# Buffers, transposes and normalisations of the first down stage in a fused attention and gated-MLP kernel

## The chip, the core and the metric

The kernel runs on one core of a Trainium2 chip. The core has five engines that run side by side and wait for one another by semaphores: TensorE (PE) for matmuls and transposes, VectorE (DVE) and ScalarE (ACT) for elementwise work, GpSimd (POOL) and SyncE (SP), which here mostly issue DMA transfers. The metric is the device time of one execution in microseconds (us), the median of several runs.

## The reference

```python
mod = (_silu(c) @ w_mod).reshape(c.shape[0], 6, 1, -1)
sa, ca, ga, sb, cb, gb = ...
h = _layernorm(x) * (1 + ca) + sa
x = x + ga * _A_ref(h, A_wqkv, A_wo)
h = _layernorm(x) * (1 + cb) + sb
x = x + gb * _B_ref(h, B_w_gate, B_w_up, B_w_down)
```

`x` is 2048 tokens by 576 in bfloat16. `_A_ref` is an attention of 32 heads of 18, in which a token sees itself and seven earlier tokens at a distance of two, with a softmax over these eight. `_B_ref` is a gated MLP: `((x @ w_gate) * (x @ w_up)) @ w_down`, 576 to 4608 and back.

## The kernel before

The tokens are cut in eight chunks of 256 for the attention and in tiles of 128 for the MLP. The MLP takes the tiles in five groups, of 2, 4, 4, 3 and 3 tiles (`GROUPS`), that is, group 0 is chunk 0 and group 1 is chunks 1 and 2. A group has a gate-up stage (`gate_up`), which makes `hh`, 36 tiles of 128 hidden features, and a down stage (`down`), which sums over those 36 rows `f`. The attention of the later chunks is laid between the matmuls of the MLP by lists written out by hand: the stage of group 0's down sums has `at0`, in which each piece of other work has the number of the row `f` behind which it is issued. TensorE, VectorE, ScalarE and the two issuing queues each execute in the order in which the code issues; nothing reorders.

The first down stage does this for two token tiles: per row `f` a matmul into `acc` (L840, 512 columns) and one into `accr` (L844, 64 columns) for each tile. Between the rows stand, for chunks 1 to 4:

- `gb_row`: the last gating row, and POOL's issues of `wd` blocks 1 and 2 and of chunk 2's neighbour values (`b_ld(2, 0)`, `b_ld(2, 1)`, L427, from `vd` into `vsh`);
- `a_ln`, `a_norm` (L262 to L272): the first layernorm of chunk 3 or 4, statistics and normalisation on VectorE, the reciprocal root on ScalarE (L267, L268); `a_norm` is followed by the load of a later chunk's rows (`load_x`, SP);
- `a_t` (L307, L294, L296): ten transposes of the normed chunk into two PSUM tiles, `tr_pA` (three of the five feature blocks) and `tr_pB` (two), and five modulated copies out of them into `hT`; the copies named in its second argument are VectorE's, the others ScalarE's. This transposed chunk is called T;
- `qkv_block(3)` (L529): chunk 3's projections, values first, and behind the values the reciprocal root of chunk 1's second layernorm;
- `av(n)`: the next `n` of chunk 2's 14 weighting pieces on VectorE; per token half four products with the attention (L501) and three pieces of sums (L508, twice, L510, L512), the last of which writes `o_sb`;
- `b_o` (L521, L523): the transposes of `o_sb` and ScalarE's copies into `oT`; `b_w(i, j)` (L685 to L688): the output projection of a token half into `pw` and `pwr`, which VectorE turns into the residual rows `x1`;
- `b_ln`, the normalisation of `x1`, and `b_t` (L307, L294, L296): the second layernorm and its T, into `h2T`, which group 1's gate-up reads. For chunk 2 the two halves go separately, `b_t(2, (0,))` behind the last row of the list and `b_t(2, (1,))` between the last sums.

All PSUM tiles, `acc`, `accr`, `pw`, `pwr`, `tr_pA`, `tr_pB`, `pp` and so on, come from one pool of eight banks; a tile that finds no free bank waits for the reader of an earlier one.

The nine blocks of `w_down` that the stage reads (four rows `f` each) come through three buffers (`wdp`). Block `f // 4 + 3` is issued by POOL behind the last row of block `f // 4`, once TensorE has read that block. The gate and up blocks of group 0 come through three buffers of `wgup` and, for its blocks 3, 4 and 8, two more of `wgx` that exist only up to the end of group 0 and that nothing uses in its down stage:

```python
wb = (wgx if g in (3, 4, NBLK - 1) else wgup).tile([P, KF, 2, NB], BF, name="wgu")
```

Of the kernel before, what the change touches and what calls it, by code (L numbers as in the profile page):

```python
# [7 lines left out]
BF = mybir.dt.bfloat16  # L8
# [10 lines left out]
P = 128  # L19
D = 576  # L20
# [26 lines left out]
def kernel(  # L47
# [112 lines left out]
    def load_wd(g):  # L160
        if g >= NG * NBLK - 4:
            return
        r0 = (g % NBLK) * FB * P
        wb = wdp.tile([P, FB, D], BF, name="wd")
        wd_blk[g] = wb
        return nc.gpsimd.dma_start(wb[:], B_w_down[r0:r0 + FB * P, :].rearrange("(k p) n -> p k n", p=P))  # L166

# [178 lines left out]
    def a_ln(i):  # L346
        x = x_in.pop(i)
        xn, rsq, norm = layernorm(lambda j: x[:, j, :], "a")
        aa[i] = dict(xn=xn, rsq=rsq, norm=norm)
# [16 lines left out]
    def a_t(i, on_dve=(0, 1, 2), between=None):  # L366
        a_tiles(i)
        hT = aa[i]["hT"]
        transposed(aa[i]["xn"], lambda m: hT[:, m, :], (0, 1), 0, between, KT if i in PAIRED else KF)(on_dve)
# [51 lines left out]
    def b_ld(i, j):  # L421
        b = bb.setdefault(i, dict(prod={}, vsh={}))
        base = HALO + i * CH + j * P - DIL * (W - 1)
        vsh = vshp.tile([P, W, DH, H], BF, name="vsh")
        vsrc = bass.AP(vd.tensor, vd.offset + base * D, [[D, P], [DIL * D, W], [1, D]])
        b["vsh"][j] = vsh
        return nc.gpsimd.dma_start(vsh[:].rearrange("p w d h -> p w (d h)"), vsrc)  # L427
# [180 lines left out]
    def qkv_block(i, between):  # L608
        q, k, qk4, v0_, v1_ = qkv_units(i, [(0, 0, 5)])[0]
        for pair in ((v0_, v1_), (q, k), (qk4,)):  # L610
            for part in range(2):
                for unit in pair:
                    unit[part]()
            if pair[0] is v0_:
                between()
# [60 lines left out]
    def b_w(i, j):  # L676
        pw = ps([P, 512], F32, "pw")
        pwr = ps([P, 64], F32, "pwr")
        parts = [(pwr, slice(512, D)), (pw, slice(0, 512))]
        if j == 0:  # L680
            parts.reverse()
        xt = x1p.tile([P, D], BF, name="x1")
        for p_t, cs in parts:
            for m in range(KT):
                nc.tensor.matmul(p_t[:], lhsT=oT[:, m, js(j)], rhs=wo[:, m, cs], start=(m == 0), stop=(m == KT - 1))  # L685
        for p_t, cs in parts:
            nc.vector.tensor_tensor(xt[:, cs], p_t[:], ga_bc[:, cs], ALU.mult)  # L687
        nc.vector.tensor_tensor(xt[:], xt[:], x_res[i][:, j, :], ALU.add)  # L688
        x1.setdefault(i, []).append(xt)

    def b_ln(i):
        x_res.pop(i)
        bb[i]["xn"], bb[i]["rsq"], bb[i]["norm"] = layernorm(lambda j: x1[i][j], "b")
# [11 lines left out]
    def b_t(i, cols=(0, 1)):  # L705
        ht, o0 = h2_of(ST * i + cols[0])
        transposed(bb[i]["xn"], lambda m: ht[:, m, o0:o0 + P * len(cols)], cols, 2)()
# [119 lines left out]
    def down(gi, hh, bg, late=nop):  # L827
        t0, t1 = GROUPS[gi]
        nj = t1 - t0
        final = gi == NG - 1  # L830
        last = FT - (2 if final else 1) * FB
        at = bg if gi == 0 else spread([(1.0, p) for p in bg], last)
        acc = [ps([P, 512], F32, "acc") for _ in range(nj - final)]
        halves = [(ps([P, CH], F32, "acc"), slice(CH * h, CH * (h + 1))) for h in range(2)] if final else []
        accr = ps([P, 2 * ST, 64], F32, "accr")

        def mm_a(f, j):
            wb = wd_blk[gi * NBLK + f // FB]
            for a, cs in [(acc[j], slice(0, 512))] if j < len(acc) else halves:
                nc.tensor.matmul(a[:], lhsT=hh[:, f, js(j)], rhs=wb[:, f % FB, cs], start=(f == 0), stop=(f == FT - 1))  # L840

        def mm_r(f, j):
            wb = wd_blk[gi * NBLK + f // FB]
            nc.tensor.matmul(accr[:, j, :], lhsT=hh[:, f, js(j)], rhs=wb[:, f % FB, 512:D],  # L844
                             start=(f == 0 and j == 0), stop=(f == FT - 1), skip_group_check=True)

        for f in range(last):
            for j in range(nj):
                mm_a(f, j)
                mm_r(f, j)  # L850
            if f % FB == FB - 1:
                load_wd(gi * NBLK + f // FB + 3)
            for piece in at[f]:
                piece()
        xs = [x1[t // ST][t % ST] for t in range(t0, t1)]
        if final:
            for j in range(nj):
                for f in range(last, FT - FB):
                    mm_r(f, j)
            for j in range(len(acc)):  # L860
                for f in range(last, FT - FB):
                    mm_a(f, j)
        for j in range(nj):
            for f in range(FT - FB, FT):
                mm_r(f, j)
        o_ts = [gup.tile([P, 512], BF, name="o_t", tag="g_sb" if j % 2 else "u_sb") for j in range(nj)]
        t_r = smp.tile([P, 2 * ST, 64], BF, name="t_r", tag="tree")
        nc.vector.tensor_tensor(t_r[:, 0:nj, :], accr[:, 0:nj, :],
                                gb_bc[:, None, 512:D].to_broadcast([P, nj, 64]), ALU.mult)
        if final:  # L870
            for j in range(nj):
                nc.vector.tensor_tensor(xs[j][:, 512:D], t_r[:, j, :], xs[j][:, 512:D], ALU.add)
            for j in range(nj):
                r0 = (t0 + j) * P
                for a, cs in [(acc[j], slice(0, 512))] if j < nj - 1 else halves:
                    for f in range(FT - FB if j < len(acc) else last, FT):
                        wb = wd_blk[gi * NBLK + f // FB]
                        nc.tensor.matmul(a[:], lhsT=hh[:, f, js(j)], rhs=wb[:, f % FB, cs], start=False, stop=(f == FT - 1))
                    nc.vector.tensor_tensor(o_ts[j][:, cs], a[:], gb_bc[:, cs], ALU.mult)
                    nc.vector.tensor_tensor(xs[j][:, cs], o_ts[j][:, cs], xs[j][:, cs], ALU.add)  # L880
                    stored = slice(0, CH) if cs.stop == CH else slice(cs.start, D)
                    nc.sync.dma_start(out_flat[r0:r0 + P, stored], xs[j][:, stored])
            return
        for j in range(nj):
            for f in range(last, FT):
                mm_a(f, j)
            if j == 0:
                late()
            nc.vector.tensor_tensor(o_ts[j][:], acc[j][:], gb_bc[:, 0:512], ALU.mult)
        for j in range(nj):  # L890
            r0 = (t0 + j) * P
            nc.vector.tensor_tensor(xs[j][:, 0:512], o_ts[j][:], xs[j][:, 0:512], ALU.add)
            nc.vector.tensor_tensor(xs[j][:, 512:D], t_r[:, j, :], xs[j][:, 512:D], ALU.add)
            nc.sync.dma_start(out_flat[r0:r0 + P, :], xs[j][:])
        load_wd(gi * NBLK + NBLK + 2)
# [267 lines left out]
    def gb_row():  # L1163
        mod_row(lambda p, k: wm5[p, k, :] if k < KF else wm5r[p, :], gb_bc, sc_bc2)()
        behind(load_wd(1), wgu_in[4])
        behind(b_ld(2, 0), wgu_in[7])
        place_pair_rows()
        load_wd(2)
        b_ld(2, 1)


    ln2 = []

    def last_ln(j):
# [5 lines left out]
        ln2[1](j)  # L1180
        ln2[2](slice(j, j + 1))

    def last_norm(j):
        ln2[3](j)

    def av(n):
        for p in av2[:n]:
            p()
        del av2[:n]

    at0 = [[] for _ in range(FT - FB)]
    for f, piece in ((0, gb_row), (0, lambda: a_ln(3)), (1, lambda: b_o(1)), (2, lambda: av(2)), (3, lambda: (a_norm(3), load_x(5))),
                     (4, lambda: b_w(1, 0)), (5, lambda: av(2)), (6, lambda: a_t(3, (0,))), (7, lambda: b_w(1, 1)), (8, lambda: av(2)),
                     (9, lambda: b_ln(1)), (10, lambda: av(1)), (11, lambda: qkv_block(3, bb[1]["rsq"])), (11, lambda: bb[1]["norm"]()), (12, lambda: av(4)),
                     (13, lambda: b_t(1)), (15, lambda: av(3)), (19, lambda: a_ln(4)), (22, lambda: b_o(2)), (23, lambda: (a_norm(4), load_x(6))),
                     (25, lambda: b_w(2, 0)), (25, lambda: last_ln(0)), (26, lambda: b_w(2, 1)), (26, lambda: last_ln(1)), (27, lambda: a_t(4, (0,))),
                     (30, lambda: last_norm(0)), (30, lambda: last_norm(1)), (31, lambda: b_t(2, (0,)))):
        at0[f].append(piece)

    dbg = {0: at0,  # L1200
# [44 lines left out]
```

## Time and profile before

| | |
|---|---|
| median of 3 runs | 556.63 us (556.52 to 557.35) |
| the profiled execution | 556.8 us, of which the span from the first to the last instruction is 555.1 us |
| TensorE busy | 543.2 us, 98% of the span |
| VectorE, ScalarE, POOL busy | 329.5 us (59%), 254.5 us (46%), 65.8 us (12%) |
| TensorE clock granted | full speed in all 40 slices of the span |
| moved by DMA | 108.40 MB, mean 195 GB/s |
| first down stage | about 88.3 to 126.6 us of the span |

A row of a timeline gives start and duration in us, engine, line, operation, output and inputs by the program's names and shapes, and the number of instructions merged in it; a bracket at its end tells how long the engine was idle before it and what ended the idle time. A row of the waits gives who waited for whom, the total, how often. A row of stretches gives the stretch, then the busy time of TensorE's matmuls, its weight loads, VectorE, ScalarE and POOL with the number of instructions, the granted clock, the DMA share and GB/s. A row of DMA issues gives the transfer, the issuing queue, the size and the time to landing.

### The profile page before, as it was taken

The numbers are of one execution on the slowest core, as the hardware profiler recorded it, in microseconds if no ns is written. First come the engines' busy times: TensorE is split into PE (matmuls) and PEld (weight loads), VectorE is DVE, ScalarE is ACT, GpSimd is POOL, SyncE is SP. The second block draws the span as 40 slices with busy tenths as digits, with TensorE's granted clock in tenths as the row PEclk, the third lists the DMA queues.
The fourth block names the chain that finished last, engine by engine and source line by source line (L and its number), as shares of the span: only waits on it lengthen the run. The fifth ranks groups of instructions, "written<-read, shape, count | busy, mean of one in ns | idle before, by whom it ended". The sixth has DMA issues, their size and how long they took to land.

```text
span 555.1 us, 14848 instructions
## 1 busy us (share of the span) xinstructions
PE 543.2 (98%) x6283; PEld 326.2 (59%) x6317; DVE 329.5 (59%) x795; ACT 254.5 (46%) x604; POOL 65.8 (12%) x98
## 2 busy tenths in 40 slices
PE   8999999989999999999999999999999999999997
PEld 5787886656544465555544445556655555565564
DVE  7888899887369763556267786444627615322202
ACT  2746665535555664212655554113556511455500
POOL 3102213121000001112000100111100022200010
PEclk9999999999999999999999999999999999999999
DMA  8999999567345844336734775435585665976021
GB/s 271 278 279 318 346 316 345 201 198 275 100 151 178 286 140 137 109 123 184 250 85 151 230 223 184 125 97 165 168 290 192 193 191 179 322 223 188 1 86 33
DMA packets 70156, 108.40 MB, mean 195 GB/s; under 512 B 3690, under 2 KB 57850, under 8 KB 70090
## 3 DMA queue, kind: packets, MB, share of 16 engines
q1 hardware_dynamic: 58832, 61.50, 36.8%
q0 software_dynamic: 11168, 45.81, 25.8%
q8 instruction: 49, 0.80, 0.6%
q14 instruction: 17, 0.14, 0.1%
q10 hardware_dynamic: 90, 0.15, 0.1%
HBM read 103.00 MB, written 4.44 MB: 194 GB/s over the span
## 4 chain that ended last, share of the span: by engine, by line
PE 83%; DMA 9%; DVE 3%; issue 2%; ACT 1%; POOL 0%; SPq 0%; POOLq 0%
PE pg L529 28%; PE pu L529 22%; PE acc L840 19%; PE pp L529 5%; PE accr L844 3%; DMA wgr<-in_B_w_gate_dram 3%; PE pw L685 2%; DMA wo<-in_A_wo_dram 2%; PE lg L448 2%; DMA wgu<-in_B_w_gate_dram 1%; DMA x_t<-in_A_x_dram 1%; DMA wd<-in_B_w_down_dram 1%; DMA wmA<-in_w_mod_dram 1%; ACT hT L296 1%; PE tr_pA L307 0%
## 5 line engine op out<-in xcount | busy, mean ns | idle before, releaser
L529 PE MATMUL pg<-h2T,wgu 64*128 64x512 bf16 (+2 forms) x1440 | 279.9, 333 | 0.0
L529 PE MATMUL pu<-h2T,wgu 64*128 64x512 bf16 (+2 forms) x1440 | 279.1, 333 | 0.0
L529 PEld LDWEIGHTS <-wgu 64*128 64x128 bf16 x2880 | 141.2, 94 | 103.1
L796 ACT CAST u_sb<-pu 128x512 bf16<-128x512 f32 (+2 forms) x180 | 90.1, 500 | 127.9 <-PE pg L529 125.9
L802 DVE TENSOR_TENSOR hh<-g_sb,u_sb 128x512 bf16<-128x512 bf16 (+2 forms) x180 | 66.7, 372 | 113.0 <-ACT g_sb L797 111.1
L840 PE MATMUL acc<-wd,hh 128*128 128x512 bf16 (+1 forms) x523 | 130.2, 372 | 1.2 <-DMA wd<-in_B_w_down_dram 1.0
L844 PE MATMUL accr<-wd,hh 128*128 128x64 bf16 x528 | 93.7, 193 | 1.1
L797 ACT CAST g_sb<-pg 128x512 bf16<-128x512 f32 (+2 forms) x180 | 91.4, 508 | 0.0
L840 PEld LDWEIGHTS <-hh 128*128 128x128 bf16 x588 | 55.2, 98 | 60.3 <-issue 1.7
L529 PE MATMUL pg<-h2T,wgr 64*128 64x512 bf16 (+2 forms) x180 | 60.1, 334 | 0.7 <-ACT h2T L296 0.5
L529 PE MATMUL pu<-h2T,wgr 64*128 64x512 bf16 (+2 forms) x180 | 60.2, 334 | 0.0
L166 POOL DMA_DIRECT2D wd<-in_B_w_down_dram x41 | 30.8, 751 | 236.0 <-PE accr L844 212.0
L844 PEld LDWEIGHTS <-hh 128*128 128x128 bf16 x576 | 51.8, 98 | 2.7 <-issue 1.1
L501 DVE TENSOR_TENSOR vsh<-vsh,attn 128x1152 bf16<-128x1152 bf16 x56 | 40.4, 750 | 0.0
L438 DVE TENSOR_TENSOR prod<-qT,kT 128x1280 bf16<-128x1280 bf16 x46 | 36.6, 816 | 4.3 <-ACT kT L364 4.3
L529 PEld LDWEIGHTS <-wgr 64*128 64x128 bf16 x360 | 17.8, 94 | 16.6 <-issue 4.1
L427 POOL DMA_DIRECT2D vsh<-vd x14 | 12.5, 897 | 109.5 <-DVE o_sb L512 71.8
L687 DVE TENSOR_TENSOR x<-pw,ga_bc 128x512 bf16<-128x512 f32 x14 | 9.7, 689 | 26.5 <-PE pw L685 26.5
L267 ACT ACTIVATE ln_rstdb<-ln_mvb,eps 128x2 f32<-128x2 f32 (+1 forms) x10 | 3.0, 299 | 46.9 <-DVE ln_mvb L264 46.9
L294 DVE TENSOR_SCALAR h2T<-tr_pA,modc 128x128 bf16<-128x128 bf16 (+1 forms) x30 | 9.5, 371 | 24.7 <-PE tr_pA L307 24.7
L296 ACT ACTIVATE h2T<-tr_pB,modc 128x256 bf16<-128x256 bf16 (+1 forms) x18 | 8.2, 518 | 30.2 <-PE tr_pB L307 30.2
L529 PE MATMUL pp<-hT,wqk 64*128 64x256 bf16 x360 | 22.0, 269 | 0.0
(220 smaller groups left out, 555.4 us busy)
## 6 DMA issues: line engine op xcount, KB each, us to landing
wd<-in_B_w_down_dram POOLq DMA_DIRECT2D x41, 576.0 KB, 4.6
wgu<-in_B_w_gate_dram SPq DMA_DIRECT2D x45, 512.0 KB, 4.6
wgu<-in_B_w_up_dram SPq DMA_DIRECT2D x45, 512.0 KB, 5.8
vsh<-vd POOLq DMA_DIRECT2D x14, 1152.0 KB, 8.9
x_r<-in_A_x_dram SPq DMA_DIRECT2D x8, 288.0 KB, 7.0
vsh<-in_B_w_down_dram POOLq DMA_DIRECT2D x4, 576.0 KB, 9.0
out_dram<-x SPq DMA_DIRECT2D x15, 144.0 KB, 4.5
x_t<-in_A_x_dram SPq DMA_DIRECT2D x7, 288.0 KB, 6.0
```

The source lines that it names most:

```text
L166: return nc.gpsimd.dma_start(wb[:], B_w_down[r0:r0 + FB * P, :].rearrange("(k p) n -> p k n", p=P))
L296: nc.scalar.activation(dst, s, ACTF.Identity, bias=modc[:, vi_shift, m:m + 1], scale=modc[:, vi_scale, m:m + 1])
L427: return nc.gpsimd.dma_start(vsh[:].rearrange("p w d h -> p w (d h)"), vsrc)
L438: nc.vector.tensor_tensor(prod[:], aa[i]["qT"][:], aa[i]["kT"][:, :, off:off + CH], ALU.mult)
L448: nc.tensor.matmul(b["lg"][H * wl:H * (wl + 1), wq, :], lhsT=ind[:, m, :], rhs=b["prod"][4 * wq + wl][:, m, :], start=(m == 0), stop=(m == ...
L501: nc.vector.tensor_tensor(v, v, at, ALU.mult)
L529: return nc.tensor.matmul(dst, lhsT=lhs, rhs=rhs, start=first, stop=last, skip_group_check=True)
L796: nc.scalar.copy(u[:, 0:N], pu[:, 0:N])
L797: nc.scalar.copy(g[:, 0:N], pg[:, 0:N])
L802: nc.vector.tensor_tensor(hh[:, f, 0:N], g[:, 0:N], u[:, 0:N], ALU.mult)
L840: nc.tensor.matmul(a[:], lhsT=hh[:, f, js(j)], rhs=wb[:, f % FB, cs], start=(f == 0), stop=(f == FT - 1))
L844: nc.tensor.matmul(accr[:, j, :], lhsT=hh[:, f, js(j)], rhs=wb[:, f % FB, 512:D], start=(f == 0 and j == 0), stop=(f == FT - 1), skip_grou ...
```

## The change

Three things are changed, all in the first down stage. The `w_down` blocks 3, 4 and 8 of group 0 go into buffers of `wgx` rather than `wdp`. Blocks 3 and 4 are issued in `gb_row`, and the blocks issued behind rows 3, 7, 11 and 15 are then 5, 6, 7 and 8; behind rows 19 and 23 nothing is issued, and from row 27 on it is as before. T of chunks 3 and 4 is copied out by ScalarE alone. T of chunk 1 is cut in two: the transposes behind row 11 (`turn`), its copies behind row 15, behind chunk 2's last sums. With that most pieces of `at0` move by some rows: both `b_w` of chunk 1 stand together ahead of `a_t(3)` at row 4, `qkv_block(3)` is at row 10, the weighting is cut 2, 2, 2, 5, 3, and `a_norm(4)` stands behind `b_w(2, 0)`.

```diff
 def load_wd(g):
...
-        wb = wdp.tile([P, FB, D], BF, name="wd")
+        wb = wgx.tile([P, FB, D], BF, name="wgu") if g in (3, 4, NBLK - 1) else wdp.tile([P, FB, D], BF, name="wd")
...
-            if f % FB == FB - 1:
-                load_wd(gi * NBLK + f // FB + 3)
+            if f % FB == FB - 1 and (gi > 0 or f // FB not in (4, 5)):
+                load_wd(gi * NBLK + f // FB + (5 if gi == 0 and f // FB < 4 else 3))
...
 def gb_row():
...
         load_wd(2)
+        load_wd(3)
         b_ld(2, 1)
+        load_wd(4)
...
+    turned = []
+
+    def turn(i):
+        ht, o0 = h2_of(ST * i)
+        turned.append(transposed(bb[i]["xn"], lambda m: ht[:, m, o0:o0 + CH], (0, 1), 2))
...
-                     (4, lambda: b_w(1, 0)), (5, lambda: av(2)), (6, lambda: a_t(3, (0,))), (7, lambda: b_w(1, 1)), (8, lambda: av(2)),
-                     (9, lambda: b_ln(1)), (10, lambda: av(1)), (11, lambda: qkv_block(3, bb[1]["rsq"])), (11, lambda: bb[1]["norm"]()), (12, lambda: av(4)),
-                     (13, lambda: b_t(1)), (15, lambda: av(3)), (19, lambda: a_ln(4)), (22, lambda: b_o(2)), (23, lambda: (a_norm(4), load_x(6))),
-                     (25, lambda: b_w(2, 0)), (25, lambda: last_ln(0)), (26, lambda: b_w(2, 1)), (26, lambda: last_ln(1)), (27, lambda: a_t(4, (0,))),
-                     (30, lambda: last_norm(0)), (30, lambda: last_norm(1)), (31, lambda: b_t(2, (0,)))):
+                     (4, lambda: b_w(1, 0)), (4, lambda: b_w(1, 1)), (4, lambda: a_t(3, ())), (5, lambda: av(2)), (8, lambda: b_ln(1)), (9, lambda: av(2)),
+                     (10, lambda: qkv_block(3, bb[1]["rsq"])), (10, lambda: bb[1]["norm"]()), (11, lambda: av(5)), (11, lambda: turn(1)),
+                     (15, lambda: av(3)), (15, lambda: turned.pop()()), (17, lambda: a_ln(4)), (19, lambda: b_o(2)), (22, lambda: b_w(2, 0)),
+                     (22, lambda: (a_norm(4), load_x(6))), (23, lambda: last_ln(0)), (23, lambda: b_w(2, 1)), (25, lambda: a_t(4, ())),
+                     (26, lambda: last_ln(1)), (30, lambda: last_norm(0)), (30, lambda: last_norm(1)), (31, lambda: b_t(2, (0,)))):
```

## The prediction

> **What bounds the kernel now.** I read the page, then TensorE's (PE's) waits, then the timelines of the first down stage, which is the only place whose code moves.
>
> ```profile
> span 555.1 us, 14848 instructions
> PE 543.2 (98%) x6283; PEld 326.2 (59%) x6317; DVE 329.5 (59%) x795; ACT 254.5 (46%) x604; POOL 65.8 (12%) x98
> ...
> PE pg L529 <- DMA wgu<-in_B_w_gate_dram: 0.2, 1, 0.2
> ...
> 88.30:126.60 38.30, 34.88 (x378) 21.88 (x381) 34.14 (x91) 17.67 (x51) 8.95 (x13) 1.00 0.74 235
> ```
>
> TensorE sets the time: 98% busy. Of its few waits behind the start all but the last in this list (0.2, the first gate-up block's) lie between 88.3 and 126.6 us, the stage that the change rewrites. There VectorE (DVE, the third figure of the stretch) is busy 34.14 of 38.30 us, so it is the next limit. The stage's fixed points on TensorE, in its timeline:
>
> ```profile
> 88.37 0.39 PE L840 MATMUL acc<-wd,hh 128*128 128x512 bf16 x1
> 92.61 1.24 PE L685 MATMUL pw<-wo,oT 128*128 128x512 bf16 x5
> 93.84 0.38 PE L840 MATMUL acc<-wd,hh 128*128 128x512 bf16 x1
> 95.43 0.34 PE L307 MATMUL tr_pA<-ident,ln_xn 128*128 128x128 bf16 x3
> 99.37 0.19 PE L844 MATMUL accr<-wd,hh 128*128 128x64 bf16 x1
> 100.48 2.38 PE L529 MATMUL pp<-wv,hT 64*128 64x288 bf16 x36 [0.92 <-ACT hT L296]
> 107.62 0.39 PE L840 MATMUL acc<-wd,hh 128*128 128x512 bf16 x1
> 109.17 0.38 PE L840 MATMUL acc<-wd,hh 128*128 128x512 bf16 x1
> 113.58 0.61 PE L521 MATMUL oT_pA<-ident,o_sb 128*128 128x128 bf16 x8
> 115.82 0.38 PE L840 MATMUL acc<-wd,hh 128*128 128x512 bf16 x1 [1.03 <-DMA wd<-in_B_w_down_dram]
> 116.80 1.24 PE L685 MATMUL pw<-wo,oT 128*128 128x512 bf16 x5
> 123.44 0.34 PE L307 MATMUL tr_pA<-ident,ln_xn 128*128 128x128 bf16 x3 [0.53 <-DVE ln_xn L272]
> 126.60 0.37 PE L529 MATMUL pg<-h2T,wgr 64*128 64x512 bf16 x1 [0.47 <-ACT h2T L296]
> ```
>
> In brackets is the idle time and who ended it. An accr's row lasts 0.19 but the next matmul starts some 0.03 behind it, so each bracket hides 0.16 more: 0.92 + 1.03 + 0.53 + 0.47 + 4 x 0.16 = 3.6 us, and 0.35 at the transposes near 95.43. That is 3.95 us to be had. The remaining 38.23 - 3.95 = 34.28 us is issue time that the change only reorders. Its units: a row f 0.49 (109.17 to 113.58 is nine), a b_w 1.23 (92.61 to 93.84), chunk 3's qkv block 7.14 (100.48 to 107.62); a b_o or a pair of transposes 0.56, gb_row 1.22.
>
> **Part 1: T of chunk 3, and a new wait.** Both b_w of chunk 1 now stand at f = 4, ahead of a_t(3). Eight PSUM banks: acc, acc, accr hold three, the two b_w four more, so tr_pA takes the last and tr_pB must wait until VectorE has emptied chunk 1's first pw. In VectorE's order that copy stands behind a_norm(3), and nothing ahead of it is changed:
>
> ```profile
> 95.49 0.68 DVE L687 TENSOR_TENSOR x<-pw,ga_bc 128x512 bf16<-128x512 f32 x1
> 96.72 1.42 DVE L501 TENSOR_TENSOR vsh<-vsh,attn 128x1152 bf16<-128x1152 bf16 x2
> 98.50 1.02 ACT L296 ACTIVATE hT<-tr_pA,modc 128x256 bf16<-128x256 bf16 x2 [4.74 <-DVE hT L294]
> ```
>
> TensorE comes to tr_pB at 92.61 + 2 x 1.23 + 0.17 = 95.24; the bank is free at 96.17 + 0.06. New wait: 0.99. Queued behind it on TensorE is everything, f = 5 on; ScalarE (ACT) waits too. In exchange hT no longer waits 4.74 for VectorE's one copy: ScalarE does all five, some 0.46 apart (two take 1.02, one 0.56) from 96.7, when tr_pA is full, and is ready at 99.1. TensorE ends a_t(3) at 96.62 and f = 10 six rows later, at 99.56, so the 0.92 wait goes. The qkv block ends at 106.70, f = 11 at 107.19: 0.43 ahead of the 107.62 for the same work.
>
> **Part 2: chunk 1's T and the sums.** VectorE's norm of chunk 1 keeps its distance to the qkv block, since ScalarE copies the values first:
>
> ```profile
> 104.25 1.19 DVE L272 TENSOR_SCALAR ln_xn<-x,ln_mvb,ln_rstdb 128x576 bf16<-128x576 bf16 x4 [0.22 <-ACT ln_rstdb L268]
> 105.34 2.76 DVE L501 TENSOR_TENSOR vsh<-vsh,attn 128x1152 bf16<-128x1152 bf16 x4
> 109.26 1.05 DVE L294 TENSOR_SCALAR h2T<-tr_pA,modc 128x256 bf16<-128x256 bf16 x3 [1.16 <-PE tr_pA L307]
> 112.47 0.46 DVE L512 TENSOR_TENSOR o_sb<-vsh 128x576 bf16<-128x576 bf16 x1
> ```
>
> 104.25 - 100.48 = 3.77, so it starts at 103.33 and ends 104.42; the last two adds of token half 0 now follow. All four adds of a half take 2.7 (110.23, where the copies end, to 112.93), these two an estimated 1.2 of it. The products start at 105.62 and take 2.7, the adds 2.7: o_sb is complete at 111.05. That is 1.9 earlier than 112.93, mostly because the 1.16 wait and 0.97 of h2T copies no longer stand between products and adds. TensorE: turn(1) 107.19 to 107.75, eight rows to 111.67, then b_o(2), whose second transpose needs o_sb: slack 0.6. turn(1)'s two banks are held until VectorE copies them at 112.0; b_o's two bring the held ones to seven, so that costs nothing.
>
> **Part 3: the buffers.** Only the order of the transfers on POOL's queue changes. The issues before, then the times to landing of the first three and of the one at 110.61:
>
> ```profile
> 90.53 0.76 POOL L166 DMA_DIRECT2D wd<-in_B_w_down_dram  x1 [5.69 <-PE pb L332]
> 91.28 0.89 POOL L427 DMA_DIRECT2D vsh<-vd  x1
> 92.58 0.76 POOL L166 DMA_DIRECT2D wd<-in_B_w_down_dram  x1 [0.41 <-PE accr L844]
> 96.67 0.75 POOL L166 DMA_DIRECT2D wd<-in_B_w_down_dram  x1 [3.33 <-PE pwr L685]
> 110.61 0.76 POOL L166 DMA_DIRECT2D wd<-in_B_w_down_dram  x1 [5.79 <-PE accr L844]
> ...
> wd<-in_B_w_down_dram POOLq DMA_DIRECT2D x1, 576.0 KB, 6.6
> vsh<-vd POOLq DMA_DIRECT2D x1, 1152.0 KB, 9.3
> wd<-in_B_w_down_dram POOLq DMA_DIRECT2D x1, 576.0 KB, 10.1
> wd<-in_B_w_down_dram POOLq DMA_DIRECT2D x1, 576.0 KB, 5.2
> ```
>
> They land at 97.1, 100.6, 102.7 and 115.8: in issue order, 3.5 us for 1152 KB (337 GB/s), 2.1 for 576. Block 6's issue at 110.61 had waited behind the qkv block; that is the 1.03 (1.19) stall. After, blocks 3, 4 and 5 go out by 94.4, block 6 behind f = 7 (98.1), block 7 behind f = 11 and the value stores (107.3, landing 112.5, used at 119), block 8 behind f = 15 (109.7, landing 115, used at 121); no down block is late. What moves back is b_ld(2,1), behind block 3: by 2.1 us, to 102.7, or 103.6 with x's load beside it, against 105.62 when the products need it: 2 us of cover. load_x(6) on SP moves with a_norm(4) to about 117.5; nothing follows it there until the stores. That matmuls read three blocks from other buffers costs nothing: the last stage reads vsh buffers at wd's pace.
>
> **Part 4: the tail.** TensorE, unhindered: b_o(2) ends 112.23, three rows to 113.70, b_w(2,0) to 114.93, a row, b_w(2,1) to 116.65, two rows, a_t(4) 117.63 to 118.19, six rows to 121.13. VectorE's chain starts 1.28 into b_w(2,0), as before:
>
> ```profile
> 118.08 0.69 DVE L687 TENSOR_TENSOR x<-pw,ga_bc 128x512 bf16<-128x512 f32 x1 [0.86 <-PE pw L685]
> 122.69 0.36 DVE L294 TENSOR_SCALAR hT<-tr_pA,modc 128x256 bf16<-128x256 bf16 x1
> 122.96 1.31 DVE L272 TENSOR_SCALAR ln_xn<-x,ln_mvb,ln_rstdb 128x576 bf16<-128x576 bf16 x4
> 125.20 0.85 DVE L294 TENSOR_SCALAR h2T<-tr_pA,modc 128x128 bf16<-128x128 bf16 x3
> 120.53 0.29 ACT L267 ACTIVATE ln_rstdb<-ln_mvb,eps 128x1 f32<-128x1 f32 x1 [4.53 <-DVE ln_mvb L264]
> 122.80 0.29 ACT L267 ACTIVATE ln_rstdb<-ln_mvb,eps 128x1 f32<-128x1 f32 x1 [1.75 <-DVE ln_mvb L264]
> 125.03 1.51 ACT L296 ACTIVATE h2T<-tr_pB,modc 128x128 bf16<-128x128 bf16 x4
> ```
>
> From 114.98 it takes 4.61 (118.08 to 122.69) plus 1.15 for a_norm(4) (1.19 in the row at 104.25, less the overlap), which now stands inside it; the hT copy at 122.69 is gone. Norm of half 0: 120.74 to 121.35, so the transposes wait 0.28, to 121.41. For half 1 ScalarE is late: it starts the first rstd at 118.6 (120.53 is 2.45 into the chain, and 1.15 more), has it 0.5 later, then does five hT copies to 121.4, then the second rstd (0.53) to 121.95. That is the price of T on ScalarE alone. Norm of half 1 ends 122.62; from there to the end of the last h2T copy it took 126.05 - 124.19 = 1.86, so 124.48, and the gate-up starts at 124.54. TensorE alone would be there at 121.41 + 2.53 = 123.94.
>
> **Sum.** 124.54 against 126.60: 2.06 us. The waits: gone 0.35 + 1.08 + 1.19, the last two 1.31 shrink to 0.28 + 0.60, new 0.99; 3.93 - 1.87 = 2.06. After 126.6 TensorE waits for nothing (the 0.2 above is the first gate-up block's), and all later loads are paced by it, so I carry the gain through. The profiled execution took 556.8 us, 0.17 above the median 556.63: forecast 554.7 for it, 554.6 at the median. Bounds: if neither the bank nor the tail holds (0.99 + 0.88), 552.7; I lean far to the chain, whose rows are this stage's own, hence 553.6 below.
>
> **Rivals.** A, slower: b_ld(2,1) late. If transfers of the queue share the engines rather than follow one another, it lands with the last. Behind 97.1 stand four down blocks (0.59 MB each), its 1.18, x's 0.29 and the value stores' 0.29: 4.1 MB (sizes by the code), at 337 GB/s until 109.3, at the stage's mean of 235 until 114.5. Every microsecond past 106.2 (105.62 and the slack of 0.6) is added; from 108.3 the gain is gone, from 109.4 it is measurably slower: 557.7 to 562.9, say 558.5. Against it: the landings in issue order above. Chance 0.06.
>
> B, VectorE held up by POOL: two more issues (1.5 us) move into 91.3 to 94.4, ahead of a_norm(3) and the bank. Held for all of it, the new wait is 2.5 and the time 556.1. Rows: the two products at 96.72, beside an issue at 96.67, took 1.42; the four at 105.34, with no issue, 2.76, so 0.04 per issue. Chance 0.05. The Trainium skill's page "GPSIMD Engine Reference", section "1. Specifications", speaks for B: POOL shares its SBUF interfaces with VectorE, with contention where VectorE has two SBUF inputs, as these products have. By that rule up to 1.5 us of the gain would go; the trace shows 0.04 an issue.
>
> C, no change: the gain is given back after 126.6 by a load that comes no earlier. Against it: no such wait of TensorE before. 556.6, chance 0.07.
>
> D, more: bank or tail wait absent, near 553.3, chance 0.06. The forecast has 0.76.
>
> **Chances.** Faster by over 0.2% (1.1 us, about what can be told from no change): forecast and D, 0.82; within: B and C, 0.12; slower: A, 0.06. The range 553.6 to 556.3 holds the forecast, most of D and B.
>
> **What would show it.** A wait of TensorE of about 1 us at a_t(3)'s tr_pB behind VectorE's x copy, no wait at the qkv block, none for wd, a wait of 0.3 before b_t(2) and 0.6 before the first gate-up of group 1, which starts near 124.5. Wrong if b_o(2) waits for o_sb, or if the qkv block starts after 100.

## The result and the profile after

| | before | after |
|---|---|---|
| median of 16 runs | 556.67 us (556.26 to 558.63) | 554.59 us (553.93 to 556.94) |
| ratio after to before | | 0.9961, 95% interval 0.9951 to 0.9971 |
| the profiled execution, its span | 556.8 us, 555.1 us | 554.21 us, 552.5 us |

The changed kernel is faster by 2.08 us at the median; the interval of the ratio is 1.6 to 2.7 us. The two profiled executions lie 2.6 us apart, within that interval.

The page of the kernel after, its list of TensorE's waits from 84 us on (who waited for whom, total, times, longest), and the busy time over the stage, in the columns explained for the kernel before:

```profile
span 552.5 us, 14851 instructions
PE 542.6 (98%) x6284; PEld 326.7 (59%) x6317; DVE 328.9 (60%) x793; ACT 255.5 (46%) x606; POOL 64.8 (12%) x98
...
PE tr_pB L307 <- DVE x L687: 0.8, 1, 0.8
PE accr L844 <- issue: 0.2, 1, 0.2
...
88.30:124.60 36.30, 35.07 (x385) 22.29 (x388) 32.98 (x88) 18.66 (x53) 11.25 (x15) 1.00 0.82 261
```

The three waits shown for the old stage are gone (hT at the projections, a `w_down` block, the norm ahead of the second T) and the one for h2T at the gate-up no longer shows in the list. One new wait is there, 0.76 at `tr_pB`. (The 0.2 at `accr` is put down to no other engine: it stands behind the projections, where the record of one matmul into `acc` is missing from the trace.) These are the stage's fixed points on TensorE, its timeline in the kernel after:

```profile
92.66 1.24 PE L685 MATMUL pw<-wo,oT 128*128 128x512 bf16 x5
95.11 0.33 PE L307 MATMUL tr_pA<-ident,ln_xn 128*128 128x128 bf16 x3
96.20 0.27 PE L307 MATMUL tr_pB<-ident,ln_xn 128*128 128x128 bf16 x2 [0.76 <-DVE x L687]
...
99.71 2.38 PE L529 MATMUL pp<-wv,hT 64*128 64x288 bf16 x36
111.83 0.61 PE L521 MATMUL oT_pA<-ident,o_sb 128*128 128x128 bf16 x8
113.86 1.24 PE L685 MATMUL pw<-wo,oT 128*128 128x512 bf16 x5
121.28 0.33 PE L307 MATMUL tr_pA<-ident,ln_xn 128*128 128x128 bf16 x3
122.94 1.03 PE L840 MATMUL acc<-wgu,hh 128*128 128x512 bf16 x4
124.00 0.37 PE L529 MATMUL pg<-h2T,wgr 64*128 64x512 bf16 x1
```

The gate-up of group 1 starts at 124.00 instead of 126.60. From the first `b_w` of chunk 1 to this start the stage takes 31.34 (124.00 - 92.66) against 33.99 (126.60 - 92.61). I use this length, called the stage below, for all kernels, since the profiled executions reach its start up to 1 us apart. The gain of 2.60 (126.60 to 124.00) is carried to the end unchanged. These two rows are the last matmuls of the program in the timelines of the kernel before and after:

```profile
547.93 3.42 PE L878 MATMUL acc<-vsh,hh 128*128 128x512 bf16 x23
```

```profile
545.33 3.42 PE L878 MATMUL acc<-vsh,hh 128*128 128x512 bf16 x23
```

### The profile page after: what moved, and what is told of

It reads as the page before. It is cut to its first block, busy times and chain, and to the rows that moved or that the text cites. A ratio compares the mean times of both kernels' runs of the same rounds, so it can differ in the third digit from the quotient of the medians.

```text
span 552.5 us, 14851 instructions
## 1 busy us (share of the span) xinstructions
PE 542.6 (98%) x6284; PEld 326.7 (59%) x6317; DVE 328.9 (60%) x793; ACT 255.5 (46%) x606; POOL 64.8 (12%) x98
## 4 chain that ended last, share of the span: by engine, by line
PE 88%; DMA 9%; DVE 2%; issue 1%; ACT 0%; SPq 0%
PE pg L529 28%; PE pu L529 22%; PE acc L840 21%; PE pp L529 6%; PE accr L844 4%; DMA wgr<-in_B_w_gate_dram 3%; PE pw L685 2%; DMA wo<-in_A_wo_dram 2%; PE lg L448 2%; DMA wgu<-in_B_w_gate_dram 1%; DMA x_t<-in_A_x_dram 1%; DMA wmA<-in_w_mod_dram 1%; PE tr_pA L307 1%; PE tr_pB L307 0%; PE oT_pA L521 0%
## 5 line engine op out<-in xcount | busy, mean ns | idle before, releaser
L840 PE MATMUL acc<-wd,hh 128*128 128x512 bf16 (+1 forms) x501 | 124.3, 371 | 0.2
L844 PE MATMUL accr<-wd,hh 128*128 128x64 bf16 x504 | 90.2, 193 | 1.2 <-issue 0.2
L166 POOL DMA_DIRECT2D wd<-in_B_w_down_dram x38 | 28.5, 751 | 229.5 <-PE accr L844 205.0
```

## The experiments

My theory after the result: (1) the order of the pieces, with the cut T of chunk 1 and the copies on ScalarE, makes the gain, and the buffers remove only the stall for block 6; (2) the wait for a PSUM bank is a true cost of the new order; (3) the tail shrank by more than forecast because a gate-up matmul waits only for the copy that it reads. The rivals stand with each run. Every ratio is against runs of the kernel before on the same chip. The intervals are 0.9 to 1.8 us wide, so the ratio tells the buffers alone, and the three runs with T two rows later taken together, from the kernel after, and none of the others. What the smaller edits are worth is read from the stage, of one profiled execution each. It came out as 31.34 in three kernels that differ only in buffers and transfers (the kernel after, the order alone, the values behind blocks 3, 4, 5), and between 30.32 and 30.37 in the three with T later.

| run | ratio to before, 95% | stage, us |
|---|---|---|
| before | | 33.99 |
| after | 0.9961 (0.9951 to 0.9971) | 31.34 |
| buffers alone | 0.9986 (0.9977 to 0.9994) | 33.07 |
| order alone | 0.9960 (0.9947 to 0.9973) | 31.34 |
| T of chunk 3 two rows later | 0.9940 (0.9928 to 0.9952) | 30.37 |
| the same, block 2 earlier | 0.9940 (0.9928 to 0.9952) | 30.32 |
| one copy of chunk 3's T on VectorE | 0.9965 (0.9950 to 0.9980) | 32.07 |
| one copy of chunk 4's T on VectorE | 0.9958 (0.9943 to 0.9973) | 31.95 |
| chunk 1's T whole | 0.9964 (0.9953 to 0.9975) | 31.59 |
| values behind blocks 3, 4, 5 | 0.9954 (0.9938 to 0.9970) | 31.34 |
| T later, no buffers | 0.9942 (0.9928 to 0.9956) | 30.34 |
| values behind block 6 | 0.9978 (0.9962 to 0.9994) | 32.54 |
| last copies reversed | 0.9967 (0.9953 to 0.9982) | 31.22, and 0.34 behind its first matmuls |

### The buffers alone

The kernel before, with the new buffers and issues, and its own lists:

```diff
+        wb = wgx.tile([P, FB, D], BF, name="wgu") if g in (3, 4, NBLK - 1) else wdp.tile([P, FB, D], BF, name="wd")
+            if f % FB == FB - 1 and (gi > 0 or f // FB not in (4, 5)):
+                load_wd(gi * NBLK + f // FB + (5 if gi == 0 and f // FB < 4 else 3))
         load_wd(2)
+        load_wd(3)
         b_ld(2, 1)
+        load_wd(4)
```

> The kernel before with the buffer part alone: blocks 3, 4 and 8 in wgx, the issues as in the changed kernel, the old order of the pieces. Theory 1 (the wait for the down block is one cause among several, and what it frees is partly eaten by the next wait): TensorE's 1.03 us wait for wd is gone, the 0.92 before the qkv block stays, and VectorE's chain from b_w(2,0) on moves by 0.86 only, since that is how long it had waited for pw; the first gate-up of group 1 starts near 125.7 instead of 126.6, 0.9 us less in all. Block 2 now lands near 98.1 and row 8 stands at 97.4, so a new wait of up to 0.6 appears there, hidden by the wait for hT. Rival (the buffers are the whole change): about 2.1 to 2.6 us less, as much as the changed kernel. Rival (the stall only moves): the same time as before.

The stage is 0.92 shorter (33.07), the time 0.14% (0.8 us), as expected. TensorE's waits and the end of its stage:

```profile
PE pp L529 <- ACT hT L296: 0.9, 1, 0.9
PE tr_pA L307 <- DVE ln_xn L272: 0.8, 1, 0.8
PE pg L529 <- ACT h2T L296: 0.4, 1, 0.4
...
122.51 0.34 PE L307 MATMUL tr_pA<-ident,ln_xn 128*128 128x128 bf16 x3 [0.77 <-DVE ln_xn L272]
125.67 0.37 PE L529 MATMUL pg<-h2T,wgr 64*128 64x512 bf16 x1 [0.39 <-ACT h2T L296]
```

The stall for `w_down` (1.03) is gone, and a part of it comes back at once where VectorE is late: the wait ahead of the second T grew from 0.53 to 0.77. The wait for block 2 that I had thought possible did not come: the block, issued at 90.52, landed 5.8 later, at 96.3.

### The order alone

The kernel after, with all blocks back in `wdp` and issued as before:

```diff
-        wb = wgx.tile([P, FB, D], BF, name="wgu") if g in (3, 4, NBLK - 1) else wdp.tile([P, FB, D], BF, name="wd")
+        wb = wdp.tile([P, FB, D], BF, name="wd")
-            if f % FB == FB - 1 and (gi > 0 or f // FB not in (4, 5)):
-                load_wd(gi * NBLK + f // FB + (5 if gi == 0 and f // FB < 4 else 3))
+            if f % FB == FB - 1:
+                load_wd(gi * NBLK + f // FB + 3)
-        load_wd(3)
-        load_wd(4)
```

> The changed kernel without its buffer part: all nine blocks in wdp, block n + 3 issued behind block n, the new order of the pieces and the new copies. Theory 1: with the qkv block at row 10, block 5 goes out at 107.8 and lands at 112.3, just when row 20 begins, and block 6 goes out at 110.3, far ahead of its row 24; so TensorE waits for no block, or some 0.2 us, and the time is within 0.3 us of the changed kernel: the new order alone would have removed the stall. Block 2 lands at 97.1, so the 0.1 us gap ahead of row 8 is gone. Rival (the buffers are needed): a wait of 1 us or more for block 5 or 6, and 1 to 1.5 us more than the changed kernel.

The whole gain is there without the buffers: the same stage to 0.01, the same two rows in the list of waits, none for a `w_down` block. Its block 6, as POOL's timeline, the DMA's time to landing and TensorE's first matmul of row 24, where the block is first read, show it:

```profile
110.81 0.76 POOL L166 DMA_DIRECT2D wd<-in_B_w_down_dram  x1 [1.75 <-PE accr L844]
...
wd<-in_B_w_down_dram POOLq DMA_DIRECT2D x1, 576.0 KB, 4.6
...
117.28 0.38 PE L840 MATMUL acc<-wd,hh 128*128 128x512 bf16 x1
```

It is issued as late as in the kernel before (110.61 there) and lands at 115.4, but both `b_w` of chunk 2 now stand ahead of row 24, so there are 1.9 us to spare. Buffers and order remove the same stall; their gains do not add.

### T of chunk 3 two rows later

```diff
-(4, lambda: a_t(3, ())), (5, lambda: av(2)), (8, lambda: b_ln(1)), (9, lambda: av(2)),
-(10, lambda: qkv_block(3, bb[1]["rsq"])), (10, lambda: bb[1]["norm"]()), (11, lambda: av(5)), (11, lambda: turn(1)),
+(5, lambda: av(2)), (6, lambda: a_t(3, ())), (8, lambda: b_ln(1)), (9, lambda: av(2)),
+(11, lambda: qkv_block(3, bb[1]["rsq"])), (11, lambda: bb[1]["norm"]()), (12, lambda: av(5)), (12, lambda: turn(1)),
```

> The changed kernel with a_t(3) behind row 6 instead of row 4, the qkv block behind row 11 instead of 10, and turn(1) and the five weighting pieces behind row 12. Theory 1 (the new wait is for a PSUM bank that VectorE frees at 96.15, and the next late thing is block 2 of the down weights, landed at 98.07): the 0.76 us wait at tr_pB is gone, TensorE does rows 5 and 6 meanwhile, then stands about 0.9 us at row 8 for block 2; the qkv block starts near 100.1 with one row more done, 0.1 us ahead of the changed kernel, and the time is within 0.2 us of it. Rival (the bank wait was the cost and block 2 comes when it is needed): the qkv block starts near 99.2, and the time is 0.8 to 1.1 us less than the changed kernel.

My theory missed here and the rival held. The list of TensorE's waits is empty from 84 us on. The stage's first `b_w`, `tr_pB` and first gate-up matmul:

```profile
92.76 1.24 PE L685 MATMUL pw<-wo,oT 128*128 128x512 bf16 x5
96.40 0.27 PE L307 MATMUL tr_pB<-ident,ln_xn 128*128 128x128 bf16 x2
123.13 0.37 PE L529 MATMUL pg<-h2T,wgr 64*128 64x512 bf16 x1
```

The stage is 0.97 shorter than in the kernel after, about what the bank had cost there: 0.76 in the bracket, and 0.92 with the 0.16 that the bracket hides, since `tr_pB` otherwise starts 0.17 behind the start of `tr_pA`'s row (107.35 to 107.52), ahead of that row's end. The ratio is 0.0021 below the kernel after's. Block 2 was no limit in this execution, but my theory had taken its landing from the kernel after (98.1); here it took 5.5 and landed at 96.2, 1.1 ahead of row 8 (97.27).

### The same, with block 2 earlier

```diff
-... if g in (3, 4, NBLK - 1) else ...
+... if g in (2, 4, 7) else ...
```

> As the run with a_t(3) two rows later, and the blocks in wgx are 2, 4 and 7 instead of 3, 4 and 8, so that block 2 waits for no buffer of gb_row and goes out near 85, behind POOL's copy of wq. Theory 1: block 2 lands near 93, no wait at tr_pB and none at row 8; the qkv block starts near 99.1 to 99.2 as soon as hT is there, with one row more done; everything behind it moves by 1.0 us and the time is 0.9 to 1.1 us less than the changed kernel, 3 us less than before. Rival (VectorE's chain sets the end of the stage whatever TensorE does): no more than 0.3 us less than the changed kernel.

Block 2 was issued at 84.8 and landed at 92.6, and stage and time stayed as they were (30.32, ratio 0.9940). So block 2's landing, for which I had expected a second limit, costs nothing that these runs show in either kernel.

### T later, without the buffers

The order alone, with the diff of the third run laid on it.

> The kernel after without its buffer part (all w_down blocks in the three buffers of wdp, each block issued as in the kernel before) and with a_t(3) two rows later, as in the third run (chunk 3's projections, the weighting and chunk 1's transposes one row later). Theory (order and place of a_t(3) make the whole gain, the buffers nothing): no TensorE wait behind 84 us, 30.4 us from the first b_w of chunk 1 to the first gate-up matmul as in the third and fourth runs, the time within 0.4 us of theirs (ratio 0.994). Rival (the buffers are needed once TensorE reaches the late rows earlier): a TensorE wait for a wd block of 0.4 us or more, most likely block 5 or 6, whose buffer comes free behind rows 11 or 15, and a time 0.4 to 1 us above the third run's.

No wait, a stage of 30.34 and a ratio of 0.9942: as the theory had it. The best version found needs no extra buffers.

### One copy of chunk 3's T on VectorE

```diff
-(4, lambda: a_t(3, ()))
+(4, lambda: a_t(3, (0,)))
```

> The changed kernel, but VectorE makes one of the five copies of T of chunk 3, as before. Theory (in this order the copy stands behind both of chunk 1's residual rows on VectorE, and ScalarE's copies wait for it): VectorE copies at about 97.9 to 98.3, ScalarE starts at 98.4 and ends near 100.2, so the qkv block starts at about 100.3 instead of 99.7 and everything behind it moves: 0.5 to 0.9 us more than the changed kernel. Rival (ScalarE does not wait for VectorE, or the qkv block has slack): the same as the changed kernel within 0.2 us.

The stage is 0.73 longer. ScalarE's and TensorE's timelines:

```profile
99.07 1.02 ACT L296 ACTIVATE hT<-tr_pA,modc 128x256 bf16<-128x256 bf16 x2 [4.63 <-DVE hT L294]
101.06 2.38 PE L529 MATMUL pp<-wv,hT 64*128 64x288 bf16 x36 [0.65 <-ACT hT L296]
```

Of the 4.63 that ScalarE waits, 1.7 pass with the transposed tile ready (its last row, 97.02 and 0.33 long, ends at 97.35), since the single copy of VectorE comes behind the x copies. In the kernel after the bracket is 2.95, all of it the wait for the tile. A wait of this kind is what the change takes away: in the kernel before it was 2.7 (from the end of the transposes at 95.77 to 98.50).

### One copy of chunk 4's T on VectorE

```diff
-(25, lambda: a_t(4, ()))
+(25, lambda: a_t(4, (0,)))
```

> The changed kernel, but VectorE makes one of the five copies of T of chunk 4, as before. Theory (VectorE comes to it only behind the second statistics, near 120.9, and ScalarE's four copies, the second rstd and the last h2T copies queue behind it): ScalarE's hT ends near 123, the second rstd near 123.5, and the first gate-up of group 1 starts 1.3 to 1.7 us later than 124.0. Rival (ScalarE, with one copy fewer, is the sooner done): 0.2 to 0.5 us less than the changed kernel. The prediction had held ScalarE's five copies to be a cost, the second rstd waiting behind them until 121.95.

The stage is 0.61 longer, less than half of what I expected, and the ratio does not tell this run from the kernel after. VectorE's copy, ScalarE's and the start of the second reciprocal root (`ln_rstdb`):

```profile
119.58 0.40 DVE L294 TENSOR_SCALAR hT<-tr_pA,modc 128x256 bf16<-128x256 bf16 x1
...
120.02 1.02 ACT L296 ACTIVATE hT<-tr_pA,modc 128x256 bf16<-128x256 bf16 x2 [0.97 <-DVE hT L294]
121.83 0.30 ACT L267 ACTIVATE ln_rstdb<-ln_mvb,eps 128x1 f32<-128x1 f32 x1
```

I had put VectorE's copy behind the second statistics; it comes ahead of them. Still the second root starts later than with five copies on ScalarE. Counted from the stage's first `b_w` (92.53 here, 92.66 in the kernel after) it is 29.30 against 28.67, that is, 0.63 later: the four copies that are left begin 1.07 later, for want of VectorE's, and only one copy of some 0.46 is saved. The prediction had called the five copies on ScalarE a price; here four and one on VectorE cost more.

### Chunk 1's T whole

`turn(1)` and its copies are again one `b_t(1)`, behind row 11:

```diff
-(11, lambda: turn(1)),
-(15, lambda: turned.pop()()),
+(11, lambda: b_t(1)),
```

> The changed kernel with T of chunk 1 in one piece behind row 11, its three VectorE copies ahead of chunk 2's last sums instead of behind them. Theory: o_sb is complete 1.0 us later, near 112.1 instead of 111.13; TensorE, at b_o(2) at 111.8, waits 0.3 us for it, and 0.2 to 0.4 us are added at the end. Rival (VectorE's chain carries all of the 1.0 us to the gate-up): 1.0 us more. Rival (nothing): the same.

The stage is 0.25 longer, as expected. VectorE's three copies (0.96) stand again ahead of chunk 2's last sums, and the transposes of `o_sb` are stretched (0.61 in the kernel after) until it is complete. VectorE and TensorE:

```profile
112.44 0.46 DVE L512 TENSOR_TENSOR o_sb<-vsh 128x576 bf16<-128x576 bf16 x1
...
112.66 0.87 PE L521 MATMUL oT_pA<-ident,o_sb 128*128 128x128 bf16 x8
```

### The neighbour values later: blocks 3, 4, 5 first

```diff
         load_wd(3)
-        b_ld(2, 1)
         load_wd(4)
...
+(3, lambda: b_ld(2, 1)), (4, lambda: b_w(1, 0)),
```

> The changed kernel with chunk 2's second value load, b_ld(2,1), issued behind down blocks 3, 4 and 5 instead of behind 3 alone. It prices the rival that the prediction gave the other sign. Theory (the queue lands in the order of issue, and the cover of the load is the 1.9 us between its landing at 103.86 and the products at 105.74): it lands 3.6 to 4 us later, near 107.7; the products wait 2 us, o_sb is complete near 113.1, TensorE waits 1.3 us at b_o(2), and the time is 1.2 to 1.6 us more than that of the changed kernel. Rival (the transfers share the engines and all land together): it lands where it did, and the time is the same.

A miss: stage and time did not change. The values, issued at 93.78, landed 12.0 later, at 105.8, and VectorE began the products at 105.97 without a wait. The rival is out as well, since the landing did move, by 1.9. The order of landing was that of issue, with the values last: 96.7, 98.4, 100.0, 101.9, 105.8. But the whole queue was early here: its first block took 5.9 where the kernel after's took 7.5, and its last transfer landed 1.3 ahead of the kernel after's last (107.1). With that execution's landings the values would have come an estimated 1.4 us late (107.1 - 90.57 behind the first issue, here at 90.81, against 105.97). So that nothing was lost is in part luck.

### The neighbour values behind block 6

```diff
+(7, lambda: b_ld(2, 1)), (8, lambda: b_ln(1)),
```

> The kernel after with the load of chunk 2's neighbour values for token half 1 (b_ld(2,1)) behind w_down block 6, that is behind row 7; two further places later than in the eighth run, which put it at 93.78 and saw it land at 105.8, just ahead of the products. This prices the slower rival of the prediction. Theory: issued near 99.6, it lands 8 to 12 us later, at 107.6 to 111.6, against 105.74 when VectorE is ready for the products; a wait of VectorE of 1.9 to 5.9, of which all but about 0.5 (the distance of b_o(2) to o_sb) is added to the stage: 31.34 becomes 32.7 to 36.7, the time 556 to 560. Rival (what is late is absorbed, since VectorE does other work or the wait at b_o(2) only takes slack from the tail): less than half of VectorE's wait appears in the stage.

This makes the lateness of the prediction's slower rival happen, though by a later issue and not by shared engines. VectorE's and TensorE's timelines:

```profile
108.01 2.77 DVE L501 TENSOR_TENSOR vsh<-vsh,attn 128x1152 bf16<-128x1152 bf16 x4 [2.18 <-DMA vsh<-vd]
113.45 0.56 PE L521 MATMUL oT_pA<-ident,o_sb 128*128 128x128 bf16 x7 [1.40 <-DVE o_sb L512]
```

The values land at 107.96 (99.36 + 8.6). VectorE waits 2.18, and TensorE 1.56, the bracket's 1.40 with the 0.16 that it hides. The stage is 1.20 longer, just under the expected range, since the bank wait was 0.28 shorter in this execution. The time is 0.17% above the kernel after's, which the intervals do not tell from nothing. TensorE waits for all of VectorE's wait but some 0.6, as the prediction had reckoned. So the price of lateness was about right; in the kernel after the values are not late, and nothing has to be paid.

### The last copies in reverse

VectorE's three copies of the last T piece go out for feature blocks 2, 1, 0:

```diff
-            for m in range(KT):
+            for m in order:
...
+        evict(order=(2, 1, 0, 3, 4) if (i, cols) == (2, (1,)) else range(KT))
```

> The kernel after with one order reversed: VectorE's three copies of the last T piece (b_t(2,(1,)), ahead of the first gate-up of group 1) are issued for feature blocks 2, 1, 0 rather than 0, 1, 2. Gate-up reads the blocks in the order 4 (ScalarE's), 0, 1, 2, 3. In the kernel after, VectorE's three copies took 123.67 to 124.50, the gate-up began at 124.00 and its matmuls of blocks 0, 1, 2 at 124.22, 124.43, 124.65, so none waited. Theory (each matmul waits for its own block's copy, not for the last copy): block 0 is now the last to be copied, at 124.50 rather than 123.95, and the second pair of gate-up matmuls waits for it: TensorE idle 0.2 to 0.4 us for VectorE's h2T behind the first pair, and the first gate-up matmul still near 124.0 (31.34 from the first b_w of chunk 1). Rival (the gate-up waits for the end of all five copies, as the prediction's last step had it, and after's early start is a gap in the records): no new wait, the same times as in the kernel after.

The first pair of gate-up matmuls starts as before, the second waits for block 0:

```profile
123.75 0.83 DVE L294 TENSOR_SCALAR h2T<-tr_pA,modc 128x128 bf16<-128x128 bf16 x3
...
124.08 0.37 PE L529 MATMUL pg<-h2T,wgr 64*128 64x512 bf16 x1
124.64 0.37 PE L529 MATMUL pg<-h2T,wgu 64*128 64x512 bf16 x1 [0.17 <-DVE h2T L294]
```

From the first to the second pair it is 0.56 here and 0.22 in the kernel after (124.00, 124.22); the three copies end 0.08 later than there (124.58, 124.50). So the theory held: a matmul waits for the copy that it reads, and not for the last of the five.

## Why the prediction was right, point by point

The sign held, and so did the mechanism up to the tail. The size at the median (554.6 forecast, 554.59 measured) is closer than the working deserves. In the profiled pair, where the terms can be read, the gain was 2.60 and the sum 2.06: the two tail waits, put at 0.88, came to 0.19 at most, while TensorE reached the tail 0.15 later than forecast. The interval of the ratio (1.6 to 2.7 us) holds both gains, so the hit to 0.01 is luck.

**Part 1, the new wait.** Forecast 0.99; the row at 96.20 has 0.76, with the hidden 0.16 it is 0.92. The releaser is the x copy that was named, and its row did not move:

```profile
95.46 0.69 DVE L687 TENSOR_TENSOR x<-pw,ga_bc 128x512 bf16<-128x512 f32 x1
...
96.68 1.48 ACT L296 ACTIVATE hT<-tr_pA,modc 128x256 bf16<-128x256 bf16 x3 [2.95 <-PE tr_pA L307]
98.04 1.02 ACT L296 ACTIVATE hT<-tr_pB,modc 128x256 bf16<-128x256 bf16 x2
```

hT is ready at 99.06 (forecast 99.1); the projections start at 99.71 without a wait for it (99.56). The run two rows later showed the wait to be a true cost, and an avoidable one.

**Part 2, the sums.** Norm of chunk 1 forecast 103.33, products 105.62, `o_sb` complete 111.05, `b_o(2)` 111.67; measured 103.48, 105.74, 111.13 and 111.83. All are late by 0.08 to 0.16, about the projections' 0.15, and `b_o(2)` does not wait.

```profile
103.48 1.19 DVE L272 TENSOR_SCALAR ln_xn<-x,ln_mvb,ln_rstdb 128x576 bf16<-128x576 bf16 x4 [0.96 <-ACT ln_rstdb L268]
105.74 2.76 DVE L501 TENSOR_TENSOR vsh<-vsh,attn 128x1152 bf16<-128x1152 bf16 x4
110.67 0.46 DVE L512 TENSOR_TENSOR o_sb<-vsh 128x576 bf16<-128x576 bf16 x1
```

**Part 3, the buffers.** Right that the 1.19 goes. The prediction put it down to the buffers alone, and that was wrong: with the new order it goes without them. It also said that no down block is late; none makes a wait in the list, but block 2, landing at 98.1, seems to have held row 8 up by 0.09 (its first matmul starts at 98.15 rather than 98.06). The cover of the neighbour values was forecast at 2 us, landing by 103.6. They landed at 103.9, in the kernel after's issues and landing times of POOL:

```profile
90.57 0.76 POOL L166 DMA_DIRECT2D wd<-in_B_w_down_dram  x1 [5.76 <-PE pb L332]
92.06 0.89 POOL L427 DMA_DIRECT2D vsh<-vd  x1
93.70 0.75 POOL L166 DMA_DIRECT2D wd<-in_B_w_down_dram  x1
...
wd<-in_B_w_down_dram POOLq DMA_DIRECT2D x1, 576.0 KB, 7.5
vsh<-vd POOLq DMA_DIRECT2D x1, 1152.0 KB, 11.8
wd<-in_B_w_down_dram POOLq DMA_DIRECT2D x1, 576.0 KB, 13.4
```

These three land at 98.1, 103.9 and 107.1, in issue order, as the argument against rival A had it.

**Part 4, the tail: the step that was off.** Up to here TensorE ran 0.15 behind the forecast: `b_w(2,0)` at 113.86 (113.70). The prediction then put a wait of 0.28 ahead of `b_t(2, (0,))` and one of 0.60 ahead of the gate-up, "so 124.48, and the gate-up starts at 124.54". The first is not there, and of the second little is left. VectorE's and ScalarE's rows of the kernel after:

```profile
120.81 0.59 DVE L272 TENSOR_SCALAR ln_xn<-x,ln_mvb,ln_rstdb 128x576 bf16<-128x576 bf16 x2
121.91 0.89 DVE L272 TENSOR_SCALAR ln_xn<-x,ln_mvb,ln_rstdb 128x576 bf16<-128x576 bf16 x2 [0.51 <-ACT ln_rstdb L268]
123.67 0.83 DVE L294 TENSOR_SCALAR h2T<-tr_pA,modc 128x128 bf16<-128x128 bf16 x3
...
121.33 0.31 ACT L267 ACTIVATE ln_rstdb<-ln_mvb,eps 128x1 f32<-128x1 f32 x1
123.15 0.81 ACT L296 ACTIVATE h2T<-tr_pB,modc 128x128 bf16<-128x128 bf16 x2 [0.58 <-PE tr_pB L307]
```

The chain of the engines was forecast well: norm of half 1 starting 121.95, here 121.91; the last h2T copy at 124.48, here 124.50. Wrong was what the gate-up waits for. Its first pair needs ScalarE's last copy, done at 123.96, the next pairs VectorE's three, which end some 0.28 apart and each just ahead of its matmul. So TensorE started at 124.00. Unhindered, by the prediction's own 2.53 from the transposes at 121.28, it would have been 123.81. Of the 0.19 between them an estimated 0.1 is still a wait, for ScalarE's copy and too short for the list: the row of `acc` ahead of the gate-up ends at 123.97, and a later gate-up, at 254.71, starts 0.07 ahead of the end of such a row and not 0.03 behind it. The rest is a step that the 2.53 had left out; ahead of the projections, where hT is long ready, it shows too (0.12 from 99.59 to 99.71, where 0.03 is usual). The row of before had named the right copy: its releaser at 126.60 was ScalarE's h2T, while I measured the distance to the end of VectorE's copies. The 0.28 fell away in the same manner: the norm of a half is two instructions (x2 in the row at 120.81), of which the first four transposes read only the wide first one; they began at 121.28, ahead of the row's end at 121.40. Both terms were counted to the end of a row that merges several instructions, and the second to that of the wrong engine's copies.

**Rivals.** A (values late): not so; made to happen, it cost 1.2 of stage. B (POOL holds VectorE): VectorE's rows from 91.18 to 95.46 stand 0.03 ahead of those of the kernel before, though two more issues lie beside them; the two products next to them are one of these:

```profile
93.08 1.37 DVE L501 TENSOR_TENSOR vsh<-vsh,attn 128x1152 bf16<-128x1152 bf16 x2
```

The issues at 92.95 and 93.70 lie beside it, and it took the 1.37 of the same row in the kernel before. The Trainium skill's page "GPSIMD Engine Reference", section "1. Specifications", names contention between POOL and VectorE with two SBUF inputs; for POOL's DMA issues no run here shows it. C (gain given back later): the gain is the same at 124 and at 545 us. D (more, 553.3): its tail half came true in the profiled execution, its bank half did not; the third run, where both do, has a ratio of 0.9940, which is 553.3 against the 556.67 of the kernel before.

## What to carry to other kernels

Where one engine is 98% busy, sum its waits with what their brackets hide, and ask of each consumer which single instruction of a merged row it reads: a chain that ends late for the last copy may be on time for the first. Bank pressure is a wait like any other: a piece that needs two PSUM banks when one is free belongs behind the row at which an earlier tile's reader is done, and two rows were worth about 1 us here. When two parts of a change aim at the same stall, run each alone; the cheaper one may do.

## What the runs showed that I had not expected

Equal transfers from the same place of a queue landed at different times: the block issued first, near 91, took 6.6 us in the kernel before, 7.5 in the kernel after, and 5.8, 6.8 and 5.5 in the first three runs. Where the cover is thin this shows up as a wait: in the profiled executions of three runs (a copy of chunk 4 on VectorE, chunk 1's T whole, values behind block 6) TensorE waited 0.4 to 0.9 us near 488 us, far from the edit, for an up block of the last gate-up. From the first of these and the third:

```profile
488.05 0.33 PE L529 MATMUL pu<-h2T,wgu 64*128 64x384 bf16 x1 [0.91 <-DMA wgu<-in_B_w_up_dram]
```

```profile
488.86 0.33 PE L529 MATMUL pu<-h2T,wgu 64*128 64x384 bf16 x1 [0.62 <-DMA wgu<-in_B_w_up_dram]
```

That block took 7.8, 7.4 and 7.6 us there, and 6.4 to 6.8 in the kernels before and after and four other runs that I read, which had no such wait. What makes it vary was not tried. It makes single executions differ by as much as the smaller of these edits, which is why the stage's length, and not the total alone, was compared.
